# Attention block on one core: half of x transposed by transfers, contraction in blocks of 128, the later scalings of V on GpSimd, and an order chosen from 24 plans

## The chip, the cores and the metric

The kernel runs on one core of a Trainium2 chip. The metric is the device time of one execution in microseconds (us); less is better. A core has five engines that run their own instruction streams: TensorE (matmuls, PE in the profile), VectorE (DVE), ScalarE (ACT), GpSimd (POOL) and SyncE (SP, which here only issues transfers).

## The reference

```python
B, S, D, H = 1, 2048, 448, 16          # bf16: x [1,2048,448], wqkv [448,1344], wo [448,448]
Dh = D // H                            # 28
qkv = (x @ wqkv).reshape(B, S, 3, H, Dh).transpose(2, 0, 3, 1, 4)
q, k, v = qkv[0], qkv[1], qkv[2]
scores = jnp.einsum("bhqd,bhkd->bhqk", q, k) * (Dh ** -0.5)
p = softmax(scores, axis=-1)
o = jnp.einsum("bhqk,bhkd->bhqd", p, v)
return o.transpose(0, 2, 1, 3).reshape(B, S, D) @ wo
```

## The kernel before

The 16 heads form four groups of four (`G`, `HG`); a head takes 32 of the 128 partitions, 28 of them data. The 2,048 queries are four chunks of 512 (`QW`), the keys 16 tiles of 128. One "set" is a head group and a query chunk; 16 sets follow each other (`ORDER`, L437). Within a set each of the four heads has 16 key tiles, so there are 1,024 score tiles of 128x512 in all.

**Two ways through the softmax.** TensorE writes scores into PSUM (L730). A tile pair goes to ScalarE, which takes the exponential of 128x1024 in one instruction (`do_exp`, L928, out `pt`). The other tiles go one by one to VectorE (`do_a`, L943): an affine pass turns the scores into int16 `I`, whose bits read as bf16 are a rough power of two. Four such tiles make a chain. Two more terms are `I` plus a constant (`SHIFT`): the second is added either by VectorE (`do_add`, L1014, out `J`) or by an accumulating transfer from GpSimd's queue onto a tile that GpSimd has filled with the constant (`far_chain`, L979, and `accumulate`, L990); the third always by VectorE. The three terms are multiplied with V and with two scaled copies of V (`WT`), made by `vs_job` (L576 to L584; the scalings are L579) on VectorE. A tile of ScalarE thus costs one matmul with V, a tile of VectorE three (`do_pv`, L1073).

**The order** is written by a planner inside the kernel. `add` puts operations with an engine, a duration, their needs and a priority into lists; a loop (L1272) moves a clock per engine forward, asks `pick_pe`, `pick_act`, `pick_dve`, `pick_pool` and `pick_sp` what to emit next, and emits it. How many tiles go to VectorE is decided by `dve_ok` (L772), from the planner's own durations: 0.904 for an exponential (`D_EXP`), 0.6 for a pass of `do_a`. `port` keeps a planned GpSimd operation and certain VectorE operations apart, and `after_shared` (L307) makes a GpSimd operation wait for the last such VectorE operation. Each engine runs its list in the order emitted.

**The head of the kernel.** x comes in four blocks of 512 rows, each by two transfers (`load_x`), then W in parts. TensorE transposes all four blocks (`xt_job`, L613 to L635: 64 transposes at L621, evacuated by ScalarE at L629 and VectorE at L627). The contraction over 448 is four steps of 112 rows (`CK`). `k_first` (L376) projects the K blocks of the first group (L298), squares them on ScalarE (L324), sums squares on TensorE (L409), and takes the maximum on VectorE (L414, L418, L420); `qn_first` (L484) gives the bound for the queries, scaled at L496. Only then can the first scores be made. Until Q's rows lie in `QP` (four transfers, L661, and two for the bound, L502), each score takes two matmuls. GpSimd clears V's tiles (L209, L210) and WO (L216), and loads wo in 16 transfers (L219). SyncE places rows of a constant in 16 transfers of 2 KB (L198), behind the loads.

**The end of a set.** VectorE copies the output (L1100), a transfer gathers the denominators, VectorE inverts them (L1109), two transfers spread them (L1114, L1120), GpSimd multiplies (L1123). The output projection (`oproj_job`) fills the last sets. After the last set its own chain runs alone (from L1305).

Of the kernel before, what the change touches and what calls it, by code (L numbers as in the profile page):

```python
# [16 lines left out]
LAT = 0.2  # L17
# [20 lines left out]

@with_exitstack
def kernel(  # L40
# [16 lines left out]
    CK = D // CC  # L57
# [11 lines left out]
    NXB = NKT // XB  # L69
    SHIFT = (0, 43, 85)  # L70
# [20 lines left out]
    NSET = G * NQC  # L91
    GH = 2
# [6 lines left out]
    out_perm = out2.rearrange("(p t) d -> p t d", t=NKT)  # L99
# [7 lines left out]
    XT = [[big.tile([CK, CC // 2, QW], BF16, name=f"XT{b}_{k}") for k in range(2)] for b in range(NXB)]  # L107
# [15 lines left out]
    xs = [big.tile([P, XB, D], BF16, name=f"xs{b}") for b in range(NXB)]  # L123
    QP = [[[big.tile([P, QW], BF16, name=f"QP{c}_{k}_{z}") for z in range(2)] for k in range(2)] for c in range(NQC)]
    OTL = [big.tile([P, QW], BF16, name=f"OTL{c}") for c in range(NQC)]

    def otile(g, c):
        if g < G - 1:
            return xs[c][:].rearrange("p t d -> p (t d)")[:, g * QW:(g + 1) * QW]
        return OTL[c][:]  # L130

    wq3 = wqkv.rearrange("(cc p) n -> p cc n", p=CK)
    x3 = x2.rearrange("(p t) c -> p t c", t=NKT)

    def load_w(t, eng):
        eng.dma_start(out=WRAW[t][:, :, 0:D], in_=wq3[:, :, t * D:(t + 1) * D])

    def load_x(b, eng, k=0, n=1):
        w = XB // n
        eng.dma_start(out=xs[b][:, k * w:(k + 1) * w, :], in_=x3[:, b * XB + k * w:b * XB + (k + 1) * w, :])  # L140

    def load_w0(t, eng):
        eng.dma_start(out=WG[t], in_=wq3[:, :, t * D:t * D + HG * Dh + WPAD])

    load_x(0, nc.sync, 0, 2)
    load_x(0, nc.scalar, 1, 2)
    for b in range(1, NXB):
        load_x(b, nc.sync, 0, 2)
        load_x(b, nc.scalar, 1, 2)
        if b == 1:  # L150
            load_w0(1, nc.sync)
            load_w0(0, nc.scalar)
    load_w(2, nc.sync)
    load_w(0, nc.sync)
    load_w(1, nc.sync)
# [21 lines left out]
    offs = wk.tile([P, 2 * QW], BF16, name="pt", bufs=NPT)[0:2, 0:QW]  # L177
# [12 lines left out]
    nc.vector.memset(offs, OFFS)  # L190
    for c in range(NQC):
        for k in range(2):
            for z in range(2):
                nc.vector.memset(QP[c][k][z][:], 0.0)
    for z in range(2):
        for c in range(NQC):
            for k in range(2):
                nc.sync.dma_start(out=QP[c][k][z][HP * k + Dh + NQC - 1 - c:P:2 * HP, :], in_=offs)  # L198
# [4 lines left out]
    for t in range(3):  # L203
        nc.gpsimd.memset(WRAW[t][:, :, D:D + WPAD], 0.0)

# [21 lines left out]
    def pair_tile(tg):  # L227
        return psum.tile([P, 2 * QW], F32, name=tg, tag=tg, bufs=1)

    def bank_tile(tg):  # L230
        return psum.tile([P, QW], F32, name=tg, tag=tg, bufs=1)


    free = {"PE": 0.0, "ACT": 0.0, "DVE": 0.0, "SP": 0.0, "POOL": 26.0}
    port = {"DVE": 0.0, "POOL": 0.0}
    evt = {}
    res = {"a0": 0.0, "a1": 0.0, "d0": 0.0, "d1": 0.0, "o": 0.0, "m": 0.0}
    ops = {"PE": [], "ACT": [], "DVE": [], "SP": [], "POOL": []}
    cnt = {"step": 0, "half": 0}
    held = {}  # L240
    cur = {"c_end": 0.0, "s": 0, "u": 0, "o": None, "oset": 0, "pv": 0, "half": 0, "o_open": False}
    parts = {}

    def add(eng, dur, emit, **k):
        op = Op(eng, dur, emit, **k)
        ops[eng].append(op)
        return op

    def ready(op):
        if cnt["step"] < op.gate or (op.acq == "m" and op.gives[0][0] == "O" and left() < OLAST):  # L250
            return None
        if op.acq == "m" and op.pri > 5 and ("KN0", NQC - 1) not in evt:
            return None
        r = 0.0
        for n in op.need:
            if n not in evt:
                return None
            t, e = evt[n]
            r = max(r, t + (0.03 if e == op.eng else LATS.get((e, op.eng), LAT)))
        if op.acq is not None:  # L260
            if res[op.acq] is None:
                return None
            r = max(r, res[op.acq])
        return r + op.lag

    def run(op, t):
        op.emit()
        if op.eng == "PE":
            note(t, op.cols)
        end = t + op.dur  # L270
        if op.eng == "PE" and main_on():
            cur["c_end"] = end
        if op.port:
            port[op.eng] = end
        for n in op.gives:
            evt[n] = (end + op.land, op.eng)
        if op.after is not None:
            op.after(end)
        if op.acq is not None:
            res[op.acq] = None  # L280
        if isinstance(op.rel, tuple):
            parts.setdefault(op.rel[0], []).append(end + LATS.get((op.eng, "PE"), LAT))
            if len(parts[op.rel[0]]) == op.rel[1]:
                res[op.rel[0]] = max(parts.pop(op.rel[0]))
        elif op.rel is not None:
            res[op.rel] = end + LATS.get((op.eng, "PE"), LAT)
        ops[op.eng].remove(op)
        return end


    KAt, QAt, sqt, kst, kmt = {}, {}, {}, {}, {}

    def mm_proj(ps, t, g, c, ccs):
        for cc in ccs:
            for i in range(HG):
                h = g * HG + i
                w = WG[t] if g == 0 else WRAW[t]
                nc.tensor.matmul(out=ps[HP * i:HP * (i + 1), :], lhsT=w[:, cc, h * Dh:h * Dh + HP],  # L298
                                 rhs=XT[c][cc // 2][:, cc % 2, :], start=(cc == 0), stop=(cc == CC - 1),
                                 tile_position=(0, HP * i))  # L300

    def quarters(out, lhsT, rhs, start, stop, **k):
        for i in range(P // HP):
            r = slice(HP * i, HP * (i + 1))
            nc.tensor.matmul(out=out[r, :], lhsT=lhsT[:, r], rhs=rhs, start=start, stop=stop, tile_position=(0, HP * i), **k)  # L305

    def after_shared(m):  # L307

        if "shared" in cur:
            tc.add_manual_dep(m.ins, cur["shared"].ins.name,  # L310
                              mybir.DependencyInfo(mybir.DependencyClass.Sync, mybir.DependencyReason.DATA),
                              reason="GpSimd's pass stays behind VectorE's")

    def new_sq(key):
        sqt[key] = wk.tile([P, QW], BF16, name="sq", tag="sq", bufs=4)
        return sqt[key]

    def square(key, src):
        t = new_sq(key)
        after_shared(nc.gpsimd.tensor_tensor(out=t[:], in0=src, in1=src, op=ALU.mult))  # L320

    def act_square(key, mask):
        t = new_sq(key)
        nc.scalar.activation(out=t[:], in_=held[key][:, 0:QW], func=ACT.Square, scale=mask[:, 0:1])  # L324

    def k_job(g, sc, bank, pri, gate=0, split=2):
        key = ("K", g, sc)
        n = CC // split

        def mm(part):  # L330
            if part == 0:
                held[key] = bank_tile(bank) if bank[0] != "a" else pair_tile(bank)
            mm_proj(held[key][:, 0:QW], 1, g, sc, range(part * n, (part + 1) * n))

        def evac():
            KAt[(g, sc)] = big.tile([P, QW], BF16, name=f"KA{sc}", tag=f"KA{sc}", bufs=2)
            src = held[key][:, 0:QW]
            nc.vector.tensor_scalar(out=KAt[(g, sc)][:], in0=src, scalar1=kmask[:, 0:1],  # L338
                                    scalar2=ones[:, 0:1], op0=ALU.mult, op1=ALU.add)

        for p in range(split):
            add("PE", n * D_WAVE, lambda p=p: mm(p), pri=pri, gate=gate, cols=448 * n,
                need=[("XT", sc, 0), ("XT", sc, 1), ("W", 1)] + ([key + (p - 1,)] if p else []), gives=[key + (p,)],
                acq=bank if p == 0 else None)
        add("DVE", 0.72, evac, need=[key + (split - 1,)], gives=[key], rel=bank, pri=pri)
        add("POOL", 1.08, lambda: square(key, KAt[(g, sc)][:]), need=[key], gives=[("ksq", g, sc)], pri=pri, port=True)

    def kn_job(g, bank, pri, gate=0):
        key = ("KN", g)

        def mm(sc):
            if sc == 0:
                held[key] = bank_tile(bank) if bank[0] != "a" else pair_tile(bank)
            quarters(held[key][:, 0:QW], maskK[:, sc, :], sqt.pop(("K", g, sc))[:], sc == 0, sc == NQC - 1)
# [1026 lines left out]
```

## Time and profile before

| what | us |
|---|---|
| median of 3 runs (361.76 to 362.11) | 361.9 |
| the profiled execution | 361.72 |
| its span in the profile | 359.9 |
| TensorE, VectorE, ScalarE, GpSimd busy | 343.1, 335.4, 341.1, 170.2 |
| first exponential starts | 19.39 |
| last exponential ends | 351.27 |

A group of instructions is shown as line, engine, operation, out<-in with shapes, count, then busy time and mean length of one in ns, then the idle time of the engine just before them and what ended it. Instructions of one engine overlap a little in the profile, so that a mean length is more than the distance from one start to the next. A timeline line is start, length, engine, line, operation; "x53" means that 53 instructions without a gap were merged, and the brackets hold the idle time before the first. A line of the chain of waits is start, length and what the chain was on.

### The profile page before, as it was taken

What the parts mean: (1) busy time and instruction counts of PE and PEld (TensorE: products, weight loads), DVE (VectorE), ACT (ScalarE), POOL (GpSimd) and SP (SyncE); (2) the same over time, 40 slices, a digit from 0 to 9 for tenths busy, and PEclk for the clock granted to TensorE, in tenths of its full rate; (3) what the DMA queues carried; (4) which work ended last, traced back from release to release, by engine and by line L of the source; (5) the groups of instructions that cost most, each with busy time, mean ns of one, the idle gap of its engine ahead of it and who ended that gap; (6) DMA issues with size and microseconds to landing.
All of it is one profiled execution on the core that took longest, in us unless ns stands there. A gap on an engine that the chain in (4) does not pass through costs nothing.

```text
span 359.9 us, 11256 instructions
## 1 busy us (share of the span) xinstructions
PE 343.1 (95%) x4520; PEld 111.3 (31%) x4521; DVE 335.4 (93%) x617; ACT 341.1 (95%) x373; POOL 170.2 (47%) x213
## 2 busy tenths in 40 slices
PE   8999999999999999999999999999889999999995
PEld 4533233332234322332232222222222222222233
DVE  8689999999989999999899999999999999999863
ACT  3789999999999999999999999999999999999991
POOL 8951353655444483545635765465546362521010
PEclk9999999999999999999999999999999999999999
DMA  8620063555636765365577646377857685672111
GB/s 242 142 47 15 21 125 86 113 107 105 135 75 129 148 124 113 89 132 108 117 143 149 120 91 137 78 152 158 177 116 156 128 176 129 142 147 66 34 51 54
DMA packets 24017, 41.17 MB, mean 114 GB/s; under 512 B 8604, under 2 KB 15004, under 8 KB 23964
## 3 DMA queue, kind: packets, MB, share of 16 engines
q0 software_dynamic: 8432, 29.24, 42.0%
q1 hardware_dynamic: 14348, 10.07, 10.3%
q10 hardware_dynamic: 1184, 1.14, 1.0%
q8 instruction: 35, 0.57, 0.6%
q14 instruction: 18, 0.15, 0.1%
HBM read 7.58 MB, written 1.96 MB: 27 GB/s over the span
## 4 chain that ended last, share of the span: by engine, by line
PE 37%; ACT 30%; DVE 23%; issue 9%; DMA 1%; DVEq 0%; ACTq 0%
ACT pt L928 30%; PE a L730 12%; DVE I L943 10%; PE o L1073 10%; PE m L305 5%; DVE J L1014 5%; PE m L298 4%; DVE V L579 2%; DVE V L566 2%; DVE KA L338 1%; PE o L643 1%; PE d L730 1%; DVE QA L460 1%; DVE o_sb L1100 1%; PE d L621 1%
## 5 line engine op out<-in xcount | busy, mean ns | idle before, releaser
L928 ACT ACTIVATE pt<-a 128x1024 bf16<-128x1024 f32 x358 | 329.7, 1129 | 2.9 <-PE a L730 1.3
L943 DVE TENSOR_SCALAR I<-d 128x512 int16<-128x512 f32 x278 | 181.0, 680 | 10.1 <-PE d L730 8.8
L730 PE MATMUL a<-QP,KA 32*128 32x512 bf16 (+1 forms) x704 | 137.3, 381 | 8.9 <-ACT pt L928 8.0
L1073 PE MATMUL o<-pt,V 128*32 128x512 bf16 x716 | 105.2, 384 | 0.0
L730 PE MATMUL d<-QP,KA 32*128 32x512 bf16 (+1 forms) x273 | 95.7, 383 | 0.8 <-DVE I L943 0.2
L730 PEld LDWEIGHTS <-KA 32*128 32x128 bf16 (+1 forms) x1041 | 46.1, 91 | 143.5 <-issue 141.7
L990 POOL DMA_DIRECT2D J<-I x55 | 49.6, 902 | 73.0 <-DVE I L943 49.6
L1073 PE MATMUL o<-J,V 128*32 128x512 bf16 x616 | 82.7, 384 | 0.0
L979 POOL MEMSET J<- 128x1024 int32 x55 | 60.1, 1094 | 36.7 <-PE d L730 12.0
L1014 DVE TENSOR_SCALAR J<-I 128x2048 int16<-128x2048 int16 x99 | 73.9, 764 | 0.6
L1073 PE MATMUL o<-I,V 128*32 128x512 bf16 x308 | 64.3, 384 | 0.1
L1073 PEld LDWEIGHTS <-V 128*32 128x32 bf16 x1640 | 30.8, 94 | 48.2 <-issue 45.1
L1123 POOL TENSOR_TENSOR xs<-o_sb,rr 128x512 bf16<-128x512 f32 x12 | 16.9, 1404 | 27.3 <-DVE J L1014 26.9
L298 PE MATMUL m<-XT,WRAW 112*32 112x512 bf16 x384 | 29.6, 384 | 0.2 <-DVE QA L460 0.2
L320 POOL TENSOR_TENSOR sq<-QA 128x512 bf16<-128x512 bf16 x15 | 16.8, 1122 | 23.1 <-DVE QA L460 17.8
L305 PE MATMUL m<-WRAW,XT 112*32 112x112 bf16 (+1 forms) x768 | 20.7, 230 | 0.3 <-DVE KA L338 0.3
L943 DVE TENSOR_SCALAR I<-m 128x512 int16<-128x512 f32 x30 | 20.3, 678 | 0.0
L320 POOL TENSOR_TENSOR sq<-KA 128x512 bf16<-128x512 bf16 x12 | 14.2, 1185 | 9.4 <-DVE J L1014 8.5
L305 PEld LDWEIGHTS <-XT 112*32 112x32 bf16 x768 | 12.3, 96 | 11.5 <-issue 11.4
L305 PE MATMUL m<-WO,xs 128*32 128x448 bf16 x156 | 12.5, 358 | 0.0
L730 PE MATMUL m<-QP,KA 32*128 32x512 bf16 (+1 forms) x30 | 11.5, 384 | 0.0
L460 DVE CAST QA<-m 128x512 bf16<-128x512 f32 x15 | 10.2, 683 | 0.7 <-PE m L298 0.7
(116 smaller groups left out, 207.3 us busy)
## 6 DMA issues: line engine op xcount, KB each, us to landing
J<-I POOLq DMA_DIRECT2D x55, 512.0 KB, 4.9
rr<-scr SPq DMA_DIRECT2D x60, 64.0 KB
QP<-QA SPq DMA_DIRECT2D x60, 28.0 KB
out_dram<-osb SPq DMA_DIRECT2D x12, 112.0 KB
WRAW<-in_wqkv_dram SPq DMA_DIRECT2D x3, 392.0 KB
xs<-in_x_dram ACTq DMA_DIRECT2D x4, 224.0 KB
xs<-in_x_dram SPq DMA_DIRECT2D x4, 224.0 KB
QP<-su SPq DMA_DIRECT2D x32, 2.0 KB
```

Of the source, the lines that this page charges most:

```text
L298: nc.tensor.matmul(out=ps[HP * i:HP * (i + 1), :], lhsT=w[:, cc, h * Dh:h * Dh + HP], rhs=XT[c][cc // 2][:, cc % 2, :], start=(cc == 0), s ...
L305: nc.tensor.matmul(out=out[r, :], lhsT=lhsT[:, r], rhs=rhs, start=start, stop=stop, tile_position=(0, HP * i), **k)
L320: after_shared(nc.gpsimd.tensor_tensor(out=t[:], in0=src, in1=src, op=ALU.mult))
L460: nc.vector.tensor_copy(out=t[:], in_=held[key][:, 0:QW])
L730: nc.tensor.matmul(out=out_ap, lhsT=KAt[(g, j // XB)][r, (j % XB) * P:(j % XB + 1) * P], rhs=q[r, :], start=(n == 0), stop=(n == len(terms ...
L928: nc.scalar.activation(out=pt[:], in_=ps[:], func=ACT.Exp, scale=LN2 / 128.0)
L943: nc.vector.tensor_scalar(out=dst, in0=pd[:], scalar1=BIAS, scalar2=0.0, op0=ALU.add, op1=ALU.max)
L979: m = nc.gpsimd.memset(ch[1][:].bitcast(I32), fill)
L990: after_shared(nc.gpsimd.dma_start(out=ch[1][:, w], in_=ch["I"][:, w], accum_op=ALU.add))
L1014: cur["shared"] = nc.vector.tensor_scalar(out=r[:, w], in0=ch["I"][:, w], scalar1=float(SHIFT[k]), scalar2=None, op0=ALU.add)
L1073: nc.tensor.matmul(out=o[HP * i:HP * (i + 1), :], lhsT=VT[e["k"]][g, j // XB][:, j % XB, HP * i:HP * (i + 1)], rhs=e["ap"], start=(SETMM[k ...
L1123: m = nc.gpsimd.tensor_tensor(out=otile(g, c), in0=st["o_sb"][:], in1=st["rr"][:], op=ALU.mult)
```

## The change

It does the following.

- Blocks 0 and 1 of x are loaded and transposed by TensorE as before (32 transposes); blocks 2 and 3 are written transposed into SBUF by three transposing transfers on SyncE's queue. The first (XE) carries columns 320 to 447 of both blocks, the others (XT) columns 0 to 383 of one block each.
- The contraction goes by 128 rows: three full steps and a fourth that overlaps the third by 64 rows, for which 64 rows of the weights are zero. Two of these clears are on VectorE, three on GpSimd.
- Rows of x within a block, and with them the rows of the output, are ordered differently (`out_at`).
- The weights of Q and K for groups 1 to 3 are loaded after Q's first rows; W for V follows the transposing transfers.
- Of the 16 placements of constant rows, 14 are issued by GpSimd, in the place of the loads of wo; these move to SyncE's queue and the clears of WO into the planned part, after group 0's queries.
- The first Q projection is planned ahead of the K blocks 2 and 3, and some PSUM banks in the head change.
- The scalings of V for group 1 and for groups 2 and 3 (16 of 24) are GpSimd's; the first group's stay on VectorE.
- The planner reckons 0.615 for a pass of `do_a`. It runs 24 times with different random shifts of two decisions and no instruction emitted, then once more with the shifts whose planned end came first.

Instruction counts of the two programs, from their orders:

| | before | after |
|---|---|---|
| exponentials on ScalarE | 358 | 360 |
| passes `I` on VectorE | 308 | 304 |
| passes `J` on VectorE | 99 | 99 |
| fills and accumulating transfers of GpSimd | 55 each | 53 each |
| scalings of V on VectorE, on GpSimd | 24, 0 | 8, 16 |
| matmuls of PV | 1,640 | 1,632 |
| transposes on TensorE | 64 | 32 |

The core of the diff (indentation aside):

```diff
-    CK = D // CC
+    CK = P
+    CT = D - CK
+    NPL = 2
+    NSEED = 24
+    D_A = 0.615
+    def out_at(c, tq, n=1):
+        o = out2[c * QW:(c + 1) * QW]
+        o = o.rearrange("(p t) d -> p t d", t=XB) if c < NPL else o.rearrange("(t p) d -> p t d", p=P)
+        return o[:, tq:tq + n, :] if n > 1 else o[:, tq, :]
+    def load_w(t, eng, n=D):
+        dst = WG[t] if n < D else WRAW[t][:, :, 0:D]
+        cols = slice(t * D, t * D + n)
+        eng.dma_start(out=dst[:, 0:CC - 1, :], in_=wqkv[0:(CC - 1) * CK, cols].rearrange("(cc p) n -> p cc n", p=CK))
+        eng.dma_start(out=dst[CC * CK - D:CK, CC - 1, :], in_=wqkv[(CC - 1) * CK:D, cols])
+    def load_x(b):
+        rows = slice(b * QW, (b + 1) * QW)
+        nc.sync.dma_start_transpose(out=XT[b][:], in_=x2[rows, 0:(CC - 1) * CK])
+    for b in range(NPL):
+        for eng, k in ((nc.sync, 0), (nc.scalar, 1)):
+            t = slice(k * XB // 2, (k + 1) * XB // 2)
+            eng.dma_start(out=xp[b][:, t, :], in_=x2[b * QW:(b + 1) * QW].rearrange("(p t) c -> p t c", t=XB)[:, t, :])
+    for t in range(2):
+        nc.vector.memset(WG[t][0:CC * CK - D, CC - 1, :], 0.0)
+    for t in (1, 0):
+        load_w(t, nc.scalar, HG * Dh + WPAD)
+    nc.sync.dma_start_transpose(out=XE[:], in_=x2[NPL * QW:S, CT:D])
+    for b in range(NPL, NXB):
+        load_x(b)
     load_w(2, nc.sync)
-    load_w(0, nc.sync)
-    load_w(1, nc.sync)
...
+    nc.gpsimd.memset(offs[:], OFFS)
+    offs_rows(0, 0, nc.sync)
...
+        nc.gpsimd.memset(WRAW[t][0:CC * CK - D, CC - 1, 0:D], 0.0)
...
-    for gg in range(G):
-        nc.gpsimd.memset(WO[:, gg, :], 0.0)
-    for h in range(H):
-        g, i = divmod(h, HG)
-        nc.gpsimd.dma_start(out=WO[HP * i:HP * i + Dh, g, :], in_=wo[h * Dh:(h + 1) * Dh, :])
+    for c in range(1, NQC):
+        offs_rows(c, 0, nc.gpsimd)
+    for c in range(NQC):
+        offs_rows(c, 1, nc.gpsimd)
...
     def vs_job(g, b, pri):
-            cur["shared"] = nc.vector.tensor_scalar(out=flat(VT[k][g, b]), in0=flat(VT[0][g, b]), scalar1=WT[k], scalar2=None, op0=ALU.mult)
+            if g == 0:
+                cur["shared"] = nc.vector.tensor_scalar(out=flat(VT[k][g, b]), in0=flat(VT[0][g, b]), scalar1=WT[k], scalar2=None, op0=ALU.mult)
+            else:
+                after_shared(nc.gpsimd.tensor_scalar(out=flat(VT[k][g, b]), in0=flat(VT[0][g, b]), scalar1=WT[k], scalar2=None, op0=ALU.mult))
-            add("DVE", 0.335 if g is None else 0.2, lambda k=k: scale(k), ...
+            add("POOL" if g != 0 else "DVE", 1.7 if g is None else 0.9 if g else 0.2, lambda k=k: scale(k), ...
...
-    QPRI = 3.15
+    QPRI = 3.05
+    for gg in range(G):
+        add("POOL", 0.5, lambda gg=gg: clear_wo(gg), need=[("QA", 0, CL)], gives=[("WZ", gg)], pri=95, port=True)
+    for h in range(H):
+        add("SP", 0.55, lambda h=h: load_wo(h), need=[("WZ", h // HG)], gives=[("WO", h)], pri=9, land=2.5)
+    for t in range(2):
+        add("SP", 1.2, lambda t=t: load_w(t, nc.sync), need=["QP00"], gives=[("W", t)], land=6.0, pri=3)
...
-        fin = max(free["DVE"], t + 0.5) + 0.62 * (len(a_fifo) + k + 1) + 1.4 + 0.6 * sum(NTERM - a[2] for a in adds)
-        return fin <= free["ACT"] + D_EXP * (len(exps) + max(0, left() // 2 - 2)) + 0.2
+        fin = max(free["DVE"], t + 0.5) + (D_A + 0.02) * (len(a_fifo) + k + 1) + 1.4 + 0.6 * sum(NTERM - a[2] for a in adds)
+        return fin <= free["ACT"] + D_EXP * (len(exps) + max(0, left() // 2 - 2)) + 0.2 + shake(0.4)
...
-        if can_add and t > adds[0][0]["at"] + AGE:
+        if can_add and t > adds[0][0]["at"] + AGE + shake(1.0):
...
+    d = Dry()
+    ends = {k: plan(d, d, d, d, d, d, k, True) for k in range(NSEED)}
+    seed = min(ends, key=lambda k: ends[k])
+    plan(nc, tc, psum, big, wk, dram, seed, False)
```

More of the change, by code (lines that the diff above doesn't have):

```diff
@@ L1 @@
+import random
 from contextlib import ExitStack
@@ L266, in run @@
[L266 to L288, printed above, removed]
@@ L291 @@
[L291 to L305, printed above, removed]
@@ L307, in after_shared @@
[L307 to L346, printed above, removed]
@@ L473, in q_job @@
-        if first:
-            add("ACT", 0.62, lambda: act_square(key, qmask), need=[key + (split - 1,)], gives=[("qsq", g, c)],
-                rel=(bank, 2), pri=pri)
-        else:
-            add("POOL", 1.08, lambda: square(key, QAt[(g, c)][:]), need=[key], gives=[("qsq", g, c)], pri=pri, port=True)
-            add("SP", 2.4 if g == 0 else 3.9, rows, need=[key, ("QZ", c, g % 2)] + ([("Oset", ORDER.index((g - 2, c)))] if g > 1 else []),
-                gives=[("QR", g, c)], land=1.6 if g == 0 else 4.0, pri=1)
@@ new lines, in put_d, with act_set @@
+        def put_d(got):
+            end = 0.0
+            for b, pd, step, ch, n, t in got:
+                end = max(end, turn(t) + D_S)
+                a_fifo.append((end + LATS[("PE", "DVE")], b, pd, step, ch, n))
+            cnt["half"] += len(got)
+            cnt["step"] = cnt["half"] // 2
+            return end
+        def act_set():
+            s = cur["s"]
+            while s < NSET and (half_left(s, 0) == 0 or half_left(s, 1) == 0):
+                s += 1
+            cur["s"] = s
+            return s
@@ L1214, in pick_dve @@
-    def pick_dve(t):
-        flush()
-        op, nxt = best("DVE", t)
-        can_add = adds and port["POOL"] <= t and add_ok(adds[0])
-        if op is None or (op.pri >= 0 and op.gives[0][0] != "V"):
-            last = not any(remain[cur["oset"]]) if cur["oset"] < NSET else False
-            if can_add and last and adds[0][0]["s"] == cur["oset"]:
+            op, nxt = best("PE", t)
+            c = pv_cands(t)
+            full, rest = waves(c)
+            last_chance = pts_used[0] >= NPT - 1 or left() == 0 or \
+                (c and not any(remain[cur["oset"]]))
```

1881 lines of the change are left out of this document (974 added, 907 removed).

## The prediction

> **What bounds the kernel now.** I read the page first, then the timeline of ScalarE, then the groups of VectorE and GpSimd by form, then the head second by second.
>
> ```profile
> span 359.9 us, 11256 instructions
> PE 343.1 (95%) x4520; PEld 111.3 (31%) x4521; DVE 335.4 (93%) x617; ACT 341.1 (95%) x373; POOL 170.2 (47%) x213
> ```
>
> Three engines are nearly full, so the shares alone don't name the bound. The timeline of ScalarE does, with the chain of waits beside it.
>
> ```profile
> 19.39 1.94 ACT L928 ACTIVATE pt<-a 128x1024 bf16<-128x1024 f32 x2 [0.68 <-PE a L730]
> ...
> 24.95 48.77 ACT L928 ACTIVATE pt<-a 128x1024 bf16<-128x1024 f32 x53 [0.25 <-PE d L730]
> ...
> 319.99 31.28 ACT L928 ACTIVATE pt<-a 128x1024 bf16<-128x1024 f32 x34 [0.16 <-PE d L730]
> ```
> ```profile
> 170.62 0.62 ACT pt L928
> 171.52 0.63 ACT pt L928
> ...
> 176.95 0.88 ACT pt L928
> ```
>
> The first exponential starts at 19.39, the last ends at 319.99 + 31.28 = 351.27, and there are 358. In the chain their starts lie 0.904 apart where nothing is late (170.62 to 176.95 is seven steps). The last one starts at 350.24 (its length is 1.02), so 357 steps take 330.9; at 0.904 they would take 322.7. The 8.1 us between are ScalarE's stalls: 1.0 in the first five steps (24.95 - 19.39 less 5 x 0.904), 7.1 later. So the span is a sum of four: head 19.4, exponentials 322.7 + 1.0, stalls 8.1, tail 359.9 - 351.3 = 8.6. VectorE, which takes the other share of the softmax, comes in only through the stalls: when it is late, a PSUM bank is late, TensorE's next scores are late, and ScalarE waits.
>
> Why VectorE is late:
>
> ```profile
> L943 DVE TENSOR_SCALAR I<-d 128x512 int16<-128x512 f32 x278 | 181.0, 680 | 10.1 <-PE d L730 8.8 <-PE m L730 0.5
> L1014 DVE TENSOR_SCALAR J<-I 128x2048 int16<-128x2048 int16 x99 | 73.9, 764 | 0.6
> L579 DVE TENSOR_SCALAR V<-V 128x1024 bf16<-128x1024 bf16 x8 | 4.6, 604 | 0.0
> L579 DVE TENSOR_SCALAR V<-V 128x512 bf16<-128x512 bf16 x16 | 4.5, 321 | 0.0
> ```
> ```profile
> 64.35 2.07 DVE L1014 TENSOR_SCALAR J<-I 128x2048 int16<-128x2048 int16 x1
> 64.51 1.35 POOL L320 TENSOR_TENSOR sq<-KA 128x512 bf16<-128x512 bf16 x1
> ...
> 133.70 1.41 POOL L979 MEMSET J<- 128x1024 int32 x1
> 134.22 1.50 DVE L579 TENSOR_SCALAR V<-V 128x1024 bf16<-128x1024 bf16 x2
> ```
>
> A shift pass J (median 685 ns) takes 2.07 us while GpSimd computes. The mean is 764, so 99 x 0.079 = 7.8 us of waiting for GpSimd. The pair of V scalings at 134.22 needs 1.50, where an undisturbed pair would need about 0.8.
>
> **The head.** First two stretches of a second-by-second table (busy TensorE, its weight loads, VectorE, ScalarE, GpSimd, then granted clock, DMA share and GB/s), then two stages of TensorE's timeline:
>
> ```profile
> 3.00:4.00 1.00, 1.00 (x4) 0.32 (x3) 0.99 (x5) 0.00 (x0) 0.92 (x4) 1.00 1.03 384
> ...
> 10.00:11.00 1.00, 1.00 (x18) 0.36 (x18) 1.00 (x2) 0.64 (x1) 0.94 (x3) 1.00 1.13 238
> ```
> ```profile
> 7.95 1.05 PE L298 MATMUL a<-XT,o_sb 112*32 112x512 bf16 x16
> 8.93 1.10 PE L621 MATMUL d<-ident,xs 128*112 128x128 bf16 x16
> ...
> 14.78 1.05 PE L298 MATMUL d<-XT,o_sb 112*32 112x512 bf16 x16
> ```
>
> The projection of the fourth K block starts at 14.78. Its square, norm, maximum, root and the scaling of the bound (L324, L409, L414, L418, L420, L496) follow, and the first exponential starts 19.39 - 14.78 = 4.61 later. Loads run at 238 to 384 GB/s (last column).
>
> **The change, part by part.** Counts come from the built program's instruction order.
>
> *Transposes of blocks 2 and 3 by transfer.* TensorE loses 32 of 64 transposes, and ScalarE and VectorE two copies each. The new order on TensorE is K0, K1, norm, Q, norm, K2, norm of Q, K3. With K0 at 7.95 + 0.25 (two more clears ahead of the warm-up, and two weight loads on ScalarE's queue that wait for x ahead of its table load, together 0.2 to 0.3), four projections of 0.98 and three norms of 0.31 (rows of L298 and L409, start to start) put K3 at 8.2 + 3.92 + 0.93 = 13.05, if block 3 has landed. Then the first exponential is at 17.66: head -1.7. The transfers carry 0.26 + 0.79 = 1.05 MB behind x (0.92 MB, in by 5.0) and beside 0.2 MB of weights: 1.25 MB at 384 or 238 GB/s are 3.3 or 5.3 us, so 8.3 to 10.3, 2.7 us before they are needed; W for V (0.39 MB) then by 12.0, needed at about 15.3. No row shows a transposing transfer. The nearest for a slow one are SyncE's sixteen 2 KB placements, 11.51 us or 0.72 each: 32 blocks of 128x128 at 0.72 would be 23 us. I take the loads' rate, since these are large reads of 256 to 768 B pieces and not tiny ones, and keep the other end as a rival.
>
> [...]
>
> *Order of the other transfers.* Fourteen of the 16 row placements go from SyncE to GpSimd's queue, in place of the 16 loads of wo there (8.5 us, 0.55 each): 14 x 0.55 = 7.7 instead of 8.5, and three clears of W rows instead of four of WO (0.49 each). That queue ends near 22 as before, and its first square is only due at 30. SyncE's queue, busy with placements from 7.63 to 19.14, can issue Q's rows some 3 us earlier; I count 0.2 of the early 1.0 stall for that, inside the stalls below. The W loads moved behind it are needed after 40; the wo loads moved among the denominators' transfers are needed near 290. Both lie under the exponentials. If that cover went, 12 loads at 0.55 would hold one set's scatter up by 6.6 us; SyncE waits 5.8 us there on average for the reciprocal (69.1 us in 12 waits), so 0.8 would be left over, for one set.
>
> *Contraction by 128 instead of 112, new row order of x and output.* The same number of matmul columns: 0. The tail's instructions are the same: 8.6, bound -0.3 to +0.3.
>
> *Softmax split.* ScalarE has 360 exponentials instead of 358: +2 x 0.904 = +1.8 on the path. VectorE has 304 passes I instead of 308, 4 x 0.60 = -2.4 (two in a row take 1.20), and 99 J as before. PV has 8 of 1,640 matmuls fewer: -0.4 on TensorE, beside.
>
> *Scalings of V.* Sixteen leave VectorE, eight of 512 columns and eight of 1024. Undisturbed they cost 8 x 0.20 + 8 x 0.33 = 4.2; with their waits (the pairs at 69.87, 111.92, 117.15 and 134.22) 6.4. On GpSimd each costs 0.54 or 1.02 at least (its clears of the same size), 1.04 or 2.1 at most (its products); I take 0.9 and 1.7, as its cast of 128 columns takes 0.30. That is 20.8 us in a 47% busy engine, 18.6 net of two fills. Its 97 computing operations (112.5 us) cost VectorE 7.8 of waits, so 18.6 more cost 1.3. VectorE: -2.4 - 6.4 + 1.3 = -7.5.
>
> What of this reaches ScalarE is the unknown. If all 7.1 us of late stalls came from the 10.0 us of port waits (7.8 + 2.2), a wait less is worth 0.7: (2.2 - 1.3) x 0.7 = 0.6. The 6.6 us of work are slack of 2%: between nothing and all later stalls, I take 1.0 with the head's 0.2, so 8.1 - 1.6 = 6.5.
>
> [...]
>
> **Sum.** 17.7 + 359 x 0.904 + 1.0 + 6.5 + 8.6 = 358.3 to 358.4, against 359.9: -1.5. The profiled execution took 361.72, 1.8 around its span, and the median is 361.9: 360.4.
>
> **The rivals.**
> - *The two added exponentials eat the head.* The slack on VectorE isn't used, stalls stay 8.1: span 360.0, time 362.0. For it: VectorE already waits 8.8 us for TensorE. Against: the stalls at 66.9 and 138 follow long J and V passes. 0.17.
> - *GpSimd's scalings hold up J (slower).* If each of 16 stops a J by 0.45, half of a short one, 7.2 of waits come for 2.2 that go: +5.0 x 0.7 = 3.5, stalls 10.6 with the slack, span 362.5, time 364.5; at the 0.74 of the four disturbed pairs about 368. It turns the sign from some 3.5 us of new waits. For it: J at 64.35. Against: each scaling waits for VectorE's last shared pass, and 97 such operations cost only 0.08 each. 0.15.
> - *The transposing transfers are late (slower).* They cost nothing until block 3 lands after 13.05, and break even at 14.8. At 0.72 a block: 5.4 + 23 = 28.4, head 33, time 375; landing at 16 gives 363. Against: the loads' rates. 0.10.
> - *VectorE's slack removes half of the stalls.* 4.0: span 355.9, time 357.9. 0.08.
>
> The forecast holds 0.50.
>
> **How the numbers follow.** A difference below 0.2% (0.7 us) can't be told from no change. Faster: 0.46 of the forecast and the last rival's 0.08, 0.54. Same: most of the first rival and the forecast's upper edge, 0.18. Slower: 0.28, from the two slow rivals and the upper edge of the first. The forecast's own range is 358.5 to 362 (stalls 4.6 to 8.1). The range 356.5 to 365.5 takes in large relief below and the J contention above; late transfers beyond 365.5 and the rest are left out.
>
> **What would show it.** The first exponential near 17.7 and K3's projection near 13.0 with block 3 landed before; 360 exponentials 0.904 apart; stalls of 6.5; J's mean at or below 780 ns; scalings on GpSimd of 0.9 and 1.7 us; no V scaling on VectorE after 30 us. TensorE waiting for a transfer before 13 us, or J's mean above 830 ns, would make the prediction wrong.

## The result, and the profile after

| what | before | after |
|---|---|---|
| median, us | 361.83 (361.4 to 362.11, 4 runs) | 366.54 (365.34 to 367.51, 4 runs) |
| ratio to before, 95% interval | 1 | 1.0132 [1.0113, 1.0151] |
| profiled execution and its span, us | 361.72, 359.9 | 365.34, 363.6 |
| TensorE, VectorE, ScalarE, GpSimd busy, us | 343.1, 335.4, 341.1, 170.2 | 336.3, 333.3, 341.6, 205.4 |

The change made the kernel 1.3% slower. Three engines do less or the same; only GpSimd does more. The profiled execution after took 365.34, 1.2 us less than the median, so the rows of the profile account for 3.6 us of the 4.7. First the head of the page of the profile after:

```profile
span 363.6 us, 11184 instructions
PE 336.3 (92%) x4486; PEld 108.2 (30%) x4486; DVE 333.3 (92%) x596; ACT 341.6 (94%) x373; POOL 205.4 (57%) x227
```

GpSimd's 35.2 us more are nearly twice the 18.6 of the prediction. Next ScalarE's timeline after (start, length, engine, line, operation, count of merged instructions, idle time before them):

```profile
17.16 1.94 ACT L982 ACTIVATE pt<-a 128x1024 bf16<-128x1024 f32 x2 [0.72 <-PE a L784]
...
81.30 49.08 ACT L982 ACTIVATE pt<-a 128x1024 bf16<-128x1024 f32 x53 [0.59 <-PE d L784]
131.11 2.98 ACT L982 ACTIVATE pt<-a 128x1024 bf16<-128x1024 f32 x3 [0.73 <-PE a L784]
134.40 13.90 ACT L982 ACTIVATE pt<-a 128x1024 bf16<-128x1024 f32 x15 [0.32 <-PE d L784]
149.16 24.45 ACT L982 ACTIVATE pt<-a 128x1024 bf16<-128x1024 f32 x26 [0.86 <-PE d L784]
174.70 1.02 ACT L982 ACTIVATE pt<-a 128x1024 bf16<-128x1024 f32 x1 [1.10 <-PE a L784]
176.21 146.78 ACT L982 ACTIVATE pt<-a 128x1024 bf16<-128x1024 f32 x160 [0.48 <-PE a L784]
323.35 31.40 ACT L982 ACTIVATE pt<-a 128x1024 bf16<-128x1024 f32 x34 [0.36 <-PE a L784]
```

The first exponential starts 2.2 us earlier than before, and the last ends at 354.75, 3.5 us later. Gaps of 0.3 to 1.1 us, each a wait for TensorE's scores, cut the row between 81 and 176 us; behind 176.21 it loses 2.5 us in 160 steps. The prediction's sum, filled in:

| term, us | before | predicted | after |
|---|---|---|---|
| first exponential starts | 19.4 | 17.7 | 17.2 |
| exponentials, (n - 1) x 0.904 + 1.0 | 323.7 | 325.5 | 325.5 |
| stalls of ScalarE | 8.1 | 6.5 | 12.0 |
| from the last exponential to the end | 8.6 | 8.6 | 8.8 |
| span | 359.9 | 358.4 | 363.6 |

The stalls are the start of the last exponential (353.71) less the first (17.16) and less 359 x 0.904. This row alone, 5.5 us over its forecast, is off by more than half a microsecond. The groups by form after (in the last one VectorE's eight scalings for the first head group) show what moved:

```profile
L997 DVE TENSOR_SCALAR I<-d 128x512 int16<-128x512 f32 x276 | 181.4, 680 | 15.0 <-PE d L784 13.0 <-PE m L784 0.4
L1068 DVE TENSOR_SCALAR J<-I 128x2048 int16<-128x2048 int16 x99 | 79.3, 824 | 0.5
L620 POOL TENSOR_SCALAR V<-V 128x1024 bf16<-128x1024 bf16 x8 | 22.8, 2850 | 2.4 <-DVE V L604 1.9
L620 POOL TENSOR_SCALAR V<-V 128x512 bf16<-128x512 bf16 x8 | 13.3, 1662 | 2.4 <-DVE J L1068 1.9
L618 DVE TENSOR_SCALAR V<-V 128x512 bf16<-128x512 bf16 x8 | 1.9, 283 | 0.0
```

A scaling of 1024 columns takes 2.85 us on GpSimd (the shortest are 2.77) and one of 512 takes 1.66 (shortest 1.48). The planner wrote its order with 1.7 and 0.9. VectorE waits longer for scores than before (13.0 us, it was 8.8), so it has not become the bound. J's mean rose from 764 to 824, that is 99 x 0.060 = 6.0 us of waits.

The head did what the prediction said. TensorE's timeline after, then SyncE's:

```profile
11.26 0.83 PE L336 MATMUL d<-XT,o_sb 128*32 128x512 bf16 x12
...
12.56 0.83 PE L336 MATMUL d<-XT,o_sb 128*32 128x512 bf16 x12
```
```profile
1.65 1.27 SPq L183 DMA_TRANSPOSE XE<-in_x_dram  x1
2.97 4.98 SPq L172 DMA_TRANSPOSE XT<-in_x_dram  x2
8.00 0.58 SPq L167 DMA_DIRECT2D WRAW<-in_wqkv_dram  x1
```

The projections of blocks 2 and 3 have no idle time before them (no bracket), so both blocks had landed by 11.26 and 12.56. In the trace the 4,096 packets of 256 B that make up the three transposing transfers lie between 4.80 and 10.26 us: 1.05 MB in 5.5 us. They hold SyncE for 6.2 us, longer than an ordinary load (0.58), but nothing there was due.

**One of the gaps, followed back.** All engines after, around 170 us, on the timeline; then the group of the matmuls that sum the squares:

```profile
165.74 5.61 POOL L620 TENSOR_SCALAR V<-V 128x1024 bf16<-128x1024 bf16 x2
...
171.28 0.95 POOL L1033 MEMSET J<- 128x1024 int32 x1
...
171.97 3.70 DVE L1068 TENSOR_SCALAR J<-I 128x2048 int16<-128x2048 int16 x3
...
172.20 2.92 POOL L358 TENSOR_TENSOR sq<-QA 128x512 bf16<-128x512 bf16 x2
173.72 0.40 PE L343 MATMUL m<-sq,maskK 128*32 128x512 bf16 x4 [1.51 <-POOL sq L358]
...
174.70 1.02 ACT L982 ACTIVATE pt<-a 128x1024 bf16<-128x1024 f32 x1 [1.10 <-PE a L784]
```
```profile
L343 PE MATMUL m<-sq,maskK 128*32 128x512 bf16 x108 | 10.8, 389 | 4.6 <-POOL sq L358 2.8 <-DVE V L604 1.2 <-DVE QA L498 0.5
```

Two scalings, planned at 3.4 us, take 5.6. The fill of `J` and two squares of Q stand behind them in GpSimd's queue. The squares start at 172.20, just behind the start of three J passes, which need 3.70 us instead of about 2 (the median of a J pass is 0.683). TensorE, whose order is fixed too, stands for 1.51 us at the matmul that sums the first square, with the scores behind it, and ScalarE then stands for 1.10. Before, that group of matmuls had 0.1 us of idle time in all; now it has 4.6. Its line before:

```profile
L305 PE MATMUL m<-sq,maskK 128*32 128x512 bf16 x108 | 10.8, 389 | 0.1
```

### The profile page after: what moved, and what is told of

It is laid out like the page before. It is cut to its first block, busy times and chain, and to the rows that moved or that the text cites. A ratio compares the mean times of both kernels' runs of the same rounds, so it can differ in the third digit from the quotient of the medians.

```text
span 363.6 us, 11184 instructions
## 1 busy us (share of the span) xinstructions
PE 336.3 (92%) x4486; PEld 108.2 (30%) x4486; DVE 333.3 (92%) x596; ACT 341.6 (94%) x373; POOL 205.4 (57%) x227
## 4 chain that ended last, share of the span: by engine, by line
PE 40%; ACT 38%; DVE 12%; issue 8%; DMA 1%; ACTq 0%; DVEq 0%
ACT pt L982 37%; PE a L784 15%; PE o L1127 11%; PE m L336 5%; DVE J L1068 5%; PE m L343 5%; DVE I L997 4%; DMA xs<-in_x_dram 1%; PE d L784 1%; PE o L343 1%; PE d L336 1%; PE a L336 1%; DVE osb L638 0%; DVE V L604 0%; ACT L191 0%
## 5 line engine op out<-in xcount | busy, mean ns | idle before, releaser
L784 PE MATMUL d<-QP,KA 32*128 32x512 bf16 x272 | 96.8, 383 | 1.0 <-DVE I L997 0.9
L1068 DVE TENSOR_SCALAR J<-I 128x2048 int16<-128x2048 int16 x99 | 79.3, 824 | 0.5
L1127 PE MATMUL o<-J,V 128*32 128x512 bf16 x608 | 77.8, 384 | 0.4 <-DVE J L1068 0.4
L1033 POOL MEMSET J<- 128x1024 int32 x53 | 57.6, 1098 | 32.6 <-PE o L1127 12.1
L620 POOL TENSOR_SCALAR V<-V 128x512 bf16<-128x512 bf16 (+1 forms) x16 | 36.1, 2256 | 4.8 <-DVE V L604 1.9
L336 PE MATMUL m<-XA,WRAW 128*32 128x512 bf16 x192 | 15.0, 384 | 1.0 <-DVE V L604 0.5
L343 PE MATMUL m<-sq,maskK 128*32 128x512 bf16 x108 | 10.8, 389 | 4.6 <-POOL sq L358 2.8
L336 PE MATMUL m<-XT,WRAW 128*32 128x512 bf16 x144 | 12.2, 386 | 0.1
L1154 DVE COPY o_sb<-o 128x512 f32<-128x512 f32 x15 | 10.2, 682 | 0.8 <-PE o L1127 0.5
```

Of the source, the lines that this page charges most:

```text
L620: after_shared(nc.gpsimd.tensor_scalar(out=flat(VT[k][g, b]), in0=flat(VT[0][g, b]), scalar1=WT[k], scalar2=None, op0=ALU.mult))
L784: nc.tensor.matmul(out=out_ap, lhsT=KAt[(g, j // XB)][r, (j % XB) * P:(j % XB + 1) * P], rhs=q[r, :], start=(n == 0), stop=(n == len(terms ...
L1033: m = nc.gpsimd.memset(ch[1][:].bitcast(I32), fill)
L1068: cur["shared"] = nc.vector.tensor_scalar(out=r[:, w], in0=ch["I"][:, w], scalar1=float(SHIFT[k]), scalar2=None, op0=ALU.add)
L1127: nc.tensor.matmul(out=o[HP * i:HP * (i + 1), :], lhsT=VT[e["k"]][g, j // XB][:, j % XB, HP * i:HP * (i + 1)], rhs=e["ap"], start=(SETMM[k ...
```

## The experiments

Two theories. *Price:* a scaling on GpSimd is 1.6 times as long as planned, and all that is behind it in the fixed orders comes late. *Rival:* the two added exponentials, the late transfers, or the choice among plans cost the time. A second rival lies within the first theory: the length itself does it, by holding up the J passes of VectorE that run at the same time, and not the lateness. The prediction and the expectations call this conflict the port, shared or held; no trace here shows a port, only VectorE's passes that take longer beside a GpSimd operation, such as the J of 2.07 us (median 0.685) beside a square at 64.51 in the kernel before. The runs were taken in several sessions, in which the median of the kernel before lay between 361.53 and 361.83; differences of 0.3 us across sessions therefore mean nothing, and the ratios are each to the kernel before of the same session.

**The scalings back on VectorE.**

```diff
-            if g == 0:
+            if True:
-            add("POOL" if g != 0 else "DVE", 1.7 if g is None else 0.9 if g else 0.2, ...
+            add("DVE", 0.335 if g is None else 0.2, ...
```

> The changed kernel with the 16 scalings of V of groups 1 to 3 back on VectorE, planned at 0.2 and 0.335 us as before; all else as changed (360 exponentials, 304 passes I, head with transfers). Theory, GpSimd's scalings make the loss: first exponential at 17.2, stalls back from 12.0 to about 8, time 361 to 362. Rival, the loss comes with the rest (the new plan, 360 exponentials, the new head): stalls stay near 12 and the time at 365 to 367.

Measured: 362.09 (361.75 to 363.28, 10 runs), ratio to before 1.001 [0.9999, 1.0022]. Stalls 8.7, J's mean 717. So the move of the 16 scalings, with the plan that goes with it, costs 4.45 us of the 4.7, and all other parts together come out near nothing: head -2.2, exponentials +1.8, stalls +0.6, tail +0.2.

**The true lengths in the plan.**

```diff
-            add("POOL" if g != 0 else "DVE", 1.7 if g is None else 0.9 if g else 0.2, ...
+            add("POOL" if g != 0 else "DVE", 2.8 if g is None else 1.5 if g else 0.2, ...
```

> The changed kernel with the scalings on GpSimd planned at the lengths that its profile shows, 1.5 and 2.8 us, in place of 0.9 and 1.7; the planner now makes 362 exponentials and 300 passes I. If the loss comes from the plan's wrong lengths (GpSimd's queue late, engines in fixed order waiting for it): stalls of 6 to 8, time 360 to 363. If it comes from the work itself, which holds the shared port whatever the plan says: stalls of 10 or more, time 365 to 368.

Measured: 364.17, ratio 1.0067 [1.0051, 1.0083], between the two expected ranges. GpSimd still spends 34.2 us in scalings, but the stalls fall to 8.4, below the 8.7 with the scalings on VectorE, and J's mean to 738. The plan pays otherwise: 362 exponentials instead of 360, 1.8 us (and 97 J passes instead of 99). About half of the loss (2.4 of 4.45 us) goes when the same work has its true length in the plan; of the stalls, all that the move had added goes, in this plan with four tiles fewer on VectorE.

**The kernel before, with only the 16 scalings moved.**

```diff
-            cur["shared"] = nc.vector.tensor_scalar(...)
+            if g == 0:
+                cur["shared"] = nc.vector.tensor_scalar(...)
+            else:
+                after_shared(nc.gpsimd.tensor_scalar(...))
-            add("DVE", 0.335 if g is None else 0.2, ...
+            add("POOL" if g != 0 else "DVE", 1.7 if g is None else 0.9 if g else 0.2, ...
```

> The kernel before with one part of the change alone: the 16 scalings on GpSimd, planned at 0.9 and 1.7 us (358 exponentials, 308 passes I as before). Theory, the scalings on GpSimd make the loss: head as before at 19.4, stalls from 8.1 to 12 or more, time 365 to 368. Rival, the loss comes with the rest of the change: 361 to 362.5.

Measured: 365.18, ratio 1.0091 [1.0074, 1.0108]; stalls 13.0, J's mean 805, scalings 35.2 us (in the profiled execution, of 366.13). The move alone costs 3.4 us in a kernel with the old head (first exponential at 18.86) and the old 358 exponentials as well. Where it costs differs: here the matmuls that sum squares stand idle for only 1.0 us, and J's waits grow by 4.1 us.

**The same order with half as many elements per scaling.**

```diff
-   tensor_scalar(out=flat(VT[k][g, b]), in0=flat(VT[0][g, b]), scalar1=WT[k], scalar2=None, op0=ALU.mult)
+   tensor_scalar(out=flat(VT[k][g, b]).bitcast(I32), in0=flat(VT[0][g, b]).bitcast(I32), scalar1=0.0, scalar2=None, op0=ALU.add)
```

> The changed kernel in the very same order of instructions, but each scaling on GpSimd is an integer addition of zero over half as many elements, 256 or 512 words in place of 512 or 1024 bf16: the factors are left out for groups 1 to 3. Theory, the length of these 16 instructions makes the loss: they take about 0.8 and 1.5 us, near what the plan reckons, stalls fall from 12.0 to 8 or less, time 360.5 to 362.5. Rival, the order itself is bad (360 exponentials, choice among 24 plans): stalls stay near 12, time 365 to 367.

Measured: 359.75 (359.38 to 359.93, 4 runs), ratio 0.9942 [0.9927, 0.9957]; stalls 6.3, J's mean 751. The two groups, and the same stretch as above on the timeline of this kernel:

```profile
L620 POOL TENSOR_SCALAR V<-V 128x512 int32<-128x512 int32 x8 | 13.4, 1805 | 1.9 <-DVE V L604 1.9
L620 POOL TENSOR_SCALAR V<-V 128x256 int32<-128x256 int32 x8 | 9.2, 1153 | 3.8 <-DVE J L1068 3.8
```
```profile
161.40 3.28 POOL L620 TENSOR_SCALAR V<-V 128x512 int32<-128x512 int32 x2
...
164.31 1.27 POOL L1033 MEMSET J<- 128x1024 int32 x1
...
165.23 2.35 POOL L358 TENSOR_TENSOR sq<-QA 128x512 bf16<-128x512 bf16 x2
...
168.34 1.92 DVE L1068 TENSOR_SCALAR J<-I 128x2048 int16<-128x2048 int16 x3
...
168.51 0.40 PE L343 MATMUL m<-sq,maskK 128*32 128x512 bf16 x4
```

Two scalings now take 3.28, about what the plan holds (3.4). The two squares end at 167.58, ahead of the three J passes, which take 1.92 instead of 3.70, and TensorE doesn't wait. The instructions stand in the same order on every engine; 6.8 us of the medians (5.5 of the two profiled spans) hang on the length of 16 of them.

**The same order with products in place of scalings.** A product with a constant column in place of the scalar. GpSimd's products of two tensors had been the upper bound in the prediction.

```diff
+    wts = {k: const.tile([P, 16], BF16, name=f"wts{k}") for k in range(1, NTERM)}
+    for k in wts:
+        nc.gpsimd.memset(wts[k][:], WT[k])
-   tensor_scalar(out=flat(VT[k][g, b]), in0=flat(VT[0][g, b]), scalar1=WT[k], scalar2=None, op0=ALU.mult)
+   tensor_tensor(out=flat(VT[k][g, b]), in0=flat(VT[0][g, b]), in1=wts[k][:, 0:1].to_broadcast([P, ...]), op=ALU.mult)
```

> The changed kernel in the same order, with each scaling on GpSimd made as a product of V with a constant column (tensor_tensor, the factor read with step 0) in place of a tensor_scalar. The squares of the same size take 1.03 us there, so I expect 1.03 and 2.05 us for 512 and 1024 columns instead of 1.48 and 2.77. If the length of these instructions against the plan is the cause, stalls fall to 6 to 8 and the time to 359.5 to 361.5, below both kernels; if the factor with step 0 makes the product as slow as the tensor_scalar, the time stays at 365 to 367. Rival, the shared port alone: 24.6 us of holding instead of 36.1, a third of the loss back at most, 364.

Measured: 360.63 (360.18 to 361.44, 8 runs), ratio 0.9977 [0.9967, 0.9987]; stalls 7.3. The groups:

```profile
L623 POOL TENSOR_TENSOR V<-V,wts 128x1024 bf16<-128x1024 bf16 x8 | 16.6, 2198 | 1.9 <-DVE V L607 1.9
L623 POOL TENSOR_TENSOR V<-V,wts 128x512 bf16<-128x512 bf16 x8 | 10.3, 1291 | 3.8 <-DVE J L1071 3.8
```

The shortest are 1.89 and 1.04. With 27.9 us of scalings (the sum of the 16 lengths, some of which overlap) the time lies between the kernels with 23.7 (359.75) and with 36.1 (366.54), and not on a line: 4.2 us more cost about 1, the next 8.2 nearly 6. The rival by which the time follows the length alone expected 364 and falls. In this order, undisturbed lengths 0.1 or 0.2 us over the plan are taken; at 0.6 and 1.1 they are not.

**Products planned at their own length** (1.05 and 2.05 in the plan).

> The same products, planned at 1.05 and 2.05 us, their expected lengths (360 exponentials, 304 passes I, another order). If the plan only has to be true: stalls at or below those of the run before, 359 to 361. If the lateness of a few tenths doesn't matter: the same as that run within 0.3%.

Measured: 361.67, ratio 1.0002 [0.9994, 1.0011], stalls 7.8, first exponential at 17.41. Better lengths didn't give a better plan here: it is 1.0 us slower than the run with products planned too short, outside the 359 to 361 of the first expectation and just inside the 0.3% of the second.

**Scalings on VectorE, 0.6 instead of 0.615 for a pass of `do_a`.**

```diff
-    D_A = 0.615
+    D_A = 0.6
```

> The changed kernel with the scalings back on VectorE and the planner's length of a pass I back at 0.6 us (358 exponentials, 308 passes I, as before). It leaves the new head and the choice among plans. If the two added exponentials eat the head's gain: 2 x 0.904 less than the run with 0.615, so 360 to 361. If VectorE needs the slack that 0.615 gave it: stalls above 10 and 362 or more.

Measured: 360.09 (359.63 to 362.05, 10 runs), ratio 0.9967 [0.9955, 0.998]; 358 exponentials, 308 passes I, stalls 8.1. Against the first experiment -2.0 us (-1.7 with the kernel before of each session taken off): the two exponentials account for 1.8. VectorE takes four passes more without more stalls.

**Scalings on VectorE, one plan without shifts** (`NSEED` 1 instead of 24).

> The changed kernel with the scalings back on VectorE and the plan without random shifts (first of the 24; 360 exponentials, 304 passes I). If the choice of the best planned end brings anything on the chip: 0.5 to 2 us slower than the run with the choice, 362.5 to 364. If the differences between plans are luck on the chip: within 0.3% of it either way.

Measured: 364.38, ratio 1.0082 [1.0066, 1.0097], stalls 10.9. Against the first experiment the choice among 24 plans is worth 2.3 us here. It also says how far the stalls of two plans of the same work may lie apart: 8.7 and 10.9.

**A late queue without long scalings.** The kernel with half as many elements, in its order, plus short idle instructions behind each scaling.

```diff
+   for _ in range(5 if g is None else 3):
+       nc.gpsimd.affine_select(out=idle[:], in_=idle[:], compare_op=ALU.not_equal, fill=1.0, base=0, pattern=[[0, 1]], channel_multiplier=1)
```

> The run with half as many elements per scaling (16 scalings of 0.85 and 1.49 us, factors left out for groups 1 to 3), in the same order, plus idle instructions of one column behind each scaling on GpSimd (three behind a short one, five behind a long one, an estimated 0.24 us each from its affine selects), so that GpSimd's queue is as late as in the changed kernel while the port it shares with VectorE is held no longer. If a late queue of GpSimd is what costs (its squares, products, fills and accumulating transfers come late), stalls return to 11 to 12 us and the time to 364 to 366.5. If the held port is what costs (J and V passes of VectorE that stand still), J's mean stays near 750 ns, stalls near 6.5 and the time at 360 to 361. In between, the two share the 6.8 us by how far the time comes back.

Measured: 365.21 (364.63 to 367.54, 5 runs), ratio 1.0105 [1.0081, 1.013]. The profiled execution took 367.54, 2.3 us more than the median, with stalls of 13.4, so its places say more than its sums. The same stretch of its timeline, and its group of matmuls that sum squares:

```profile
170.22 1.49 POOL L622 TENSOR_SCALAR V<-V 128x512 int32<-128x512 int32 x1
...
171.67 1.20 POOL L624 TENSOR_SCALAR_AFFINE_SELECT idle<-idle 128x1 f32<-128x1 f32 x5
...
172.81 0.95 POOL L1038 MEMSET J<- 128x1024 int32 x1
...
173.72 2.48 POOL L360 TENSOR_TENSOR sq<-QA 128x512 bf16<-128x512 bf16 x2
173.78 3.59 DVE L1073 TENSOR_SCALAR J<-I 128x2048 int16<-128x2048 int16 x3
...
174.81 0.40 PE L345 MATMUL m<-sq,maskK 128*32 128x512 bf16 x4 [0.79 <-POOL sq L360]
```
```profile
L345 PE MATMUL m<-sq,maskK 128*32 128x512 bf16 x108 | 10.8, 389 | 4.5 <-POOL sq L360 2.8 <-DVE V L606 1.1 <-DVE QA L500 0.5
```

The scalings are as short as in the kernel with half the elements, and the loss is back, with the same signature: the squares collide with the three J passes (3.59), and the matmuls that sum squares wait 4.5 us, 2.8 of them for the squares. Of the 6.8 us, 5.5 come back (365.21 against 359.75). Where the exponentials lose time against the kernel with half the elements (difference of their starts, first exponential taken as zero):

| between exponentials | the change | late queue | products |
|---|---|---|---|
| 60 and 75 | 1.2 | 3.1 | 0.3 |
| 118 and 128 | 1.6 | 0.9 | 0.5 |
| 136 and 145 | 1.2 | 1.1 | -0.1 |
| 160 and 172 | 1.9 | 1.2 | 0.0 |
| all others | -0.2 | 0.9 | 0.3 |

Four places, each of which begins during a scaling or within 5 us of the end of one, make up the whole 5.7 of the change, and the late queue loses at the same four. Only the last of them is followed back above. At the first, two J passes take 0.4 us too long over a scaling, and TensorE waits 0.82 us for a square (at 80.26); at the third it waits 1.21 us for a V of VectorE that stands behind slow J passes (at 148.12); at the second, two J passes stand behind a scaling itself. Two lines of the change's timeline there, four J passes in 4.17 us instead of about 2.5 (three took 1.92 above):

```profile
121.59 6.24 POOL L620 TENSOR_SCALAR V<-V 128x1024 bf16<-128x1024 bf16 x2
124.22 4.17 DVE L1068 TENSOR_SCALAR J<-I 128x2048 int16<-128x2048 int16 x4
```

How much is lateness and how much is holding, J's own waits show: for every J pass that is more than 0.12 us over the median, the excess, put to the GpSimd operation that overlaps it most (products of the output, 0.5 us or less, are left out).

| J's excess over, us | before | half as many elements | the change | late queue |
|---|---|---|---|---|
| squares | 4.4 | 3.3 | 6.5 | 6.1 |
| fills | 3.6 | 3.0 | 4.7 | 4.6 |
| the scalings (and idle instructions) | 0 | 0 | 2.5 | 1.2 |

In the same order, the change has 4.9 us more over squares and fills and 2.5 over the scalings. The late queue brings back nearly all of the first (4.4) and half of the second. So lateness is enough for most of a loss of this size. It isn't shown to be all: the idle instructions aren't free of the conflict either, as some groups of five took 1.48 or 2.33 us instead of 1.2, and two J passes stood 0.6 us behind them.

**Products with 0.6 in the planner**, planned short (0.9 and 1.7) and at their own length (1.05 and 2.05).

> The changed kernel with the 16 scalings as products with a constant column (1.04 and 1.89 us) still planned at 0.9 and 1.7, and 0.6 instead of 0.615 for a pass of I in the planner, which gives 358 exponentials. If the number of exponentials adds to the rest as it did with the scalings on VectorE (-2.0), the time is 358.5 to 359.5, the fastest of all. If VectorE, with four more passes of I and GpSimd's longer scalings beside it, gives it back as stalls, 360 to 362.

> As the run before, but with the products planned at their measured 1.05 and 2.05. The plan has 360 exponentials again. If planned lengths near the true ones help the order, 359.5 to 360.5 (as with products planned short); if the plan's length of a scaling matters less than the plan that happens to be chosen, anywhere from 360 to 363.

Measured: planned short 359.07 (357.97 to 360.34, 5 runs), ratio 0.993 [0.991, 0.995], 358 exponentials, stalls 7.4; at their own length 360.65 (360.46 to 361.08, 9 runs), ratio 0.997 [0.9958, 0.9982], 360 exponentials, stalls 7.4. The difference of 1.6 is nearly the two exponentials, though the plans also differ in J passes (101 and 96). The first has the lowest median of all, 0.7% below the kernel before and 2.0% below the change (359.07 / 366.54).

## Why the prediction was wrong

The forecast was 360.4 and the time 366.54, beyond the range, and of the other sign.

**The step that failed** is "On GpSimd each costs 0.54 or 1.02 at least (its clears of the same size), 1.04 or 2.1 at most (its products); I take 0.9 and 1.7". Measured: 1.48 and 2.77 undisturbed, 36.1 us for the sixteen instead of 20.8. Already the upper bound was wrong. I held an operation with one tensor and a scalar to be no dearer than one with two tensors; the profile before has no such operation of GpSimd on a large tile, so nothing showed it. The cast of 128 columns at 0.30 misled: above the 0.10 of a clear of one column it gives 1.6 ns a column, which leads to 0.9 and 1.7, and the scalings took 2.5 ns for each further column (1.29 us for 512). The planner makes the same error with the same numbers, and that is what turns it into a loss: with 16 instructions of nearly the planned length in the same order (359.75) the forecast's sum holds.

**What the longer scalings cost** was mis-sized a second time, in "Its 97 computing operations (112.5 us) cost VectorE 7.8 of waits, so 18.6 more cost 1.3". GpSimd's 35.2 us more cost 6.0, 0.17 for each microsecond and not 0.07. Those 97 stood where the planner had put them, apart from the J passes. An operation that slips does not stay there, as the table of J's excess shows: most of what the change adds in the same order lies over squares and fills. A rate read off a planned order did not hold here for work that breaks the plan. The sum also let GpSimd reach ScalarE through VectorE alone. With 6.0 in place of 1.3, its own rate of 0.7 gives 3.3 us more, stalls of 9.8 and not 12.0; it has no term for TensorE standing at the matmuls that sum squares, 4.6 us where it was 0.1. How much of the other 2.2 us comes from there was not worked out.

**The head** was right: K's last projection at 12.56 (predicted 13.05) and the first exponential at 17.16 (17.66). The half microsecond lies in its start: the first K projection was put at 8.2 and came at 7.74, and what was added behind it holds to 0.05. The transfers were in time, as blocks 2 and 3 are used without a wait at 11.26 and 12.56, and the rival of late transfers fell. Beside 0.2 MB of weights, their packets took 5.5 us and ended at 10.26; the prediction had 3.3 or 5.3 us and 8.3 to 10.3.

**The two exponentials** at 1.8 were right: 1.7 to 2.0 between the runs with 0.615 and with 0.6, at stalls of 8.7 and 8.1.

**The slack on VectorE**, 1.6 us less stalls, can't be called shown. The kernel with short scalings has 6.3, as forecast; the products have 7.3 to 7.8, and the plan chosen moves the stalls by 2.2 with no change of work.

**The tail** is 0.15 longer, within its bound, and what lies around the span is 1.8 as before.

**The rivals.** The first, two exponentials that eat the head's gain, describes the kernel with the scalings back on VectorE: 362.09 at stalls of 8.7, where it said 362.0 at 8.1. The second, scalings that hold up J, came nearest in its numbers: 7.2 of new waits, stalls 10.6 and 364.5 to 368 were its numbers, 6.0, 12.0 and 366.5 the measured ones. Its mechanism was only in part the right one. It spoke of J passes that a scaling stops. Nine J passes of the change lie over a scaling: four of them take 1.08 to 1.51 us, 2.5 too much in all, and five take 0.63 to 0.69, as ever. One that took 1.51 started at 124.83 and another, of 0.68, at 126.27; both ended while the scaling that starts at 124.42 still ran, until 127.84, as far as the profile's spans on GpSimd, which are rough, can tell. So neither stood until the scaling's end. Beside the square at 64.51 in the kernel before it was otherwise: that J pass ended 0.56 us after the square. The greater part of J's added waits (4.9 of 7.4 in the same order) comes a queue later, from squares and fills that slip onto J passes, and beside it TensorE's matmuls wait for squares. The rival's argument against it, that each scaling waits for VectorE's last shared pass, was no protection: `after_shared` keeps a GpSimd operation from starting over an earlier pass, and says nothing of the pass that comes next. "J's mean above 830 ns" was the bound set for a wrong prediction; it stands at 824, so that test was set too wide, while the test of 0.9 and 1.7 us for a scaling failed at once. The last rival, half of the stalls gone, fell with the forecast.

What stays open: how much the long scalings would cost without lateness. No run has them with a punctual queue in the same order. The plan with true lengths comes nearest, in another order and with two exponentials more: its stalls are 8.4, and J's excess over scalings is 0.4 us.

## What to carry to other kernels

In an order that is fixed ahead, an instruction that overruns its planned length can make late not only its own reader but all that stands behind it in its queue and, by the next wait, the other engines' queues (here two scalings of 5.6 us for a planned 3.4, then waits of 1.51 us on TensorE and 1.10 on ScalarE); cost it by what follows it, and measure one instance before moving sixteen. Where the trace has no instruction of the same operation on the same engine and size, the nearest rows need not bound it from above (here 1.04 us by the products, and 1.48 measured), and the range should say so. Look for another instruction with the same result: here a product with a constant column in place of a scalar turns 366.5 into 360.6 in the same order of all other instructions.

## What was not expected of the hardware

On GpSimd, the product of a bf16 tile with a scalar was slower than its product with a broadcast column: 1.48 against 1.04 us for 128x512, 2.77 against 1.89 for 128x1024 (the shortest of each). Adding a scalar to int32 words took 0.85 for 256 and 1.49 for 512 columns. Each further column took 2.5 ns both in the product with a scalar, on elements of 2 bytes ((2.77 - 1.48) / 512), and in the addition, on elements of 4 ((1.49 - 0.85) / 256). A J pass that fell on a scaling was not always held up until its end: two passes, of 1.51 and 0.68 us, ended at 126.34 and 126.95 while one ran (124.42 to 127.84), and the scaling took 3.41 us instead of 2.77. The transposing transfers occupied SyncE's queue for 1.27 us (0.26 MB) and 4.98 (two of 0.39 MB), against 0.58 for a load of weights (0.34 MB).
